# Attention products on parts of the matmul array, and the first layer's fold in plain float32

## The chip, the cores and the metric

The kernel runs on one core of one Trainium2 chip. The metric is device time in microseconds from launch to end, as a median over runs. A core has a matmul engine (TensorE: PE in the profile, its weight loads PEld), VectorE (DVE), ScalarE (ACT), GpSimd (POOL) and SyncE (SP), which here issues most DMAs; GpSimd issues the rest.

## The reference

Attention with landmarks for 4 batches of 8 heads, 576 tokens and 64 elements a head, then two MLPs over the 2304 tokens:

```python
q_lm, k_lm = means of q, k over 18 tokens each           # 32 landmarks
A  = softmax(scale * q    @ k_lm^T)                       # 576 x 32
Bm = softmax(scale * q_lm @ k_lm^T)                       # 32 x 32
C  = softmax(scale * q_lm @ k^T)                          # 32 x 576
Z  = Bm^T / (norm1(Bm) * norminf(Bm) + 1e-6)
for _ in range(6): Z = 2 * Z - Z @ Bm @ Z
attn = A @ Z @ C @ v
x = attn as (2304 tokens, 512)
x = (sigmoid(x @ w_gate) * (x @ w_val)) @ w_out           # 512 -> 1536 -> 512
x = h = x @ w_in2; (max(h, 0) + alpha * min(h, 0)) @ w_out2   # 512 -> 2048 -> 512
```

q, k and v come in float32, the MLPs' weights as 64-bit floats, which the kernel turns into float32 by integer operations on their bits.

## The kernel before

**Precision.** The MLP products run in float32r, a float32 format that TensorE takes in one go. Each operand is split into a high part and a rest (`split`: a copy on ScalarE, a subtraction on VectorE or GpSimd), and three products of such parts (`TERMS`) stand for one float32 product. The attention's products run in plain float32; each of them appears as two instructions in the trace.

**Attention.** A group is four heads of a batch (`j` = 0 or 1), a pair is two heads whose 64 elements fill the 128 partitions. `transposed` makes `qT` and `kT` of a pair: [(head, d), 576 tokens and 32 landmark means]. The scores of four heads are products over all 128 partitions: `blockdiag` spreads a pair's landmarks over the columns of its heads with the mask `lmask`, zeros elsewhere, and `pair_product` adds up the two pairs' products (`psb`, `psc`, `psa` in PSUM). `value_product` then multiplies by v, head after head, six token blocks each, into four strips of 32 partitions of `psv`. `newton` finds Z for four heads in four diagonal parts (`psz`), and multiplies it by C v (`psm`). The result goes through `lmask` into `mf`, which is block diagonal, and is split into `mhl`.

**The fold.** A @ (Z C v) @ W is computed as A @ (Z C v W). For batch b and chunk c of the weights (256 columns of w_gate and 256 of w_val), `fold` multiplies `mhl` by the chunk: per group, 3 terms by 2 pairs, six float32r products of 512 columns (`psf`). The result is split into `We[b, c, j]`. For batches 2 and 3 one `fold_two` per group and chunk does both: block-diagonal halves of one `mf` hold one batch each; batch 3's result is stored to DRAM (`we3d`) and fetched later.

**Weights of the first MLP.** A raw tile of 64-bit floats is loaded, `narrow` makes float32 of it (two operations on ScalarE and two on VectorE for w_gate and w_val, one and three for w_out), `split` makes `wconv`: 24 tiles of w_gate and w_val and 12 of w_out. The rest is subtracted on GpSimd, or on VectorE for the indices in `LO_DVE`. The 24 are stored to DRAM in split form (`wgvd`, issued by SP) and loaded again (`reload`, issued by GpSimd) for batch 1, and for batches 2 and 3. Split tiles live in 27 slots (`N_SLOT`).

**Order.** A loop of 96 steps `at` (24 for each batch) issues one `layer1` (`gv`, 12 products of 288 columns), one `layer2` of two steps before (`acc`, 12 products), and beside them conversions (batch 0), steps of the next batches' attentions, reloads (at `RELOAD_AT`), folds (at `FOLD_AT`) and, after the last fold, conversions of the second MLP's weights. A planner then orders each engine's instructions by their priority, which is mostly program order, and by when it reckons operands and buffers ready; the engines run them in that order. PSUM has eight banks: two for `gv`, four for `acc`, and two (`att`) for all attention products and folds; for batches 2 and 3 `layer1` uses `att` for odd f. The second MLP follows (`h`, `o`).

Of the kernel before, what the change touches and what calls it, by code (L numbers as in the profile page):

```python
# [21 lines left out]
def tile_landmark_attention_glu_prelu(  # L22
# [36 lines left out]
    RELOAD_AT, FOLD_AT = (16, 40), ((19, 20, 22, 23, 25, 27), (44, 46, 47, 49, 51, 53))  # L59
# [14 lines left out]
        (c, pr): dpool.tile([P, 2, NW], F32R, name=f"wgvd{c}_{pr}", tag=f"wgvd{c}_{pr}")  # L74
        for c in range(NCH)
        for pr in range(NK)
# [12 lines left out]
    lmask = cpool.tile([P, 2, 4, LM], F32, name="lmask")  # L89
    nc.gpsimd.memset(lmask, 0.0)  # L90
    for u in range(2):
        for hh in range(2):
            nc.gpsimd.memset(lmask[64 * hh : 64 * hh + 64, u, 2 * u + hh, :], 1.0)
    # eye[(h, l), l'] = 1 where l = l'
# [28 lines left out]
    def narrow(raw, to=None, act=False):  # L123
        """float32 of float64 bits, in place: sign, exponent less its bias' difference, 23
        mantissa bits. The high word, read as a float32, holds the exponent's upper eight bits in
        its own exponent: the scale takes 112 * 8 = 1023 - 127 off, and flushes what is too small."""
# [3 lines left out]
        if act:  # L130
            # the upper three of 16 bits, rounded to a whole number
# [26 lines left out]
    def load_pair_tok(src, b, pr, nm):  # L158
        """the two heads of a token side by side"""
# [14 lines left out]
    def pair_of(b, j, u):  # L174
        """the pair of heads in place u of group j; the last batch has them the other way round"""
        return 2 * j + (1 - u if b == B - 1 else u)
# [37 lines left out]
    def blockdiag(b, x, u, nm):  # L214
        t = apool.tile([P, 4, LM], F32, tag="bd", name=nm, bufs=7)
        (nc.gpsimd if b == 0 and nm[0] == "k" else nc.vector).tensor_tensor(
            out=t, in0=x[:, None, S:].to_broadcast([P, 4, LM]), in1=lmask[:, u], op=ALU.mult
        )
        return t.rearrange("p a l -> p (a l)")

    def pair_product(ps, lhsT, rhs, c0, c1):
        for u in range(2):
            nc.tensor.matmul(  # L223
                ps[:, : c1 - c0], lhsT=lhsT[u], rhs=rhs[u][:, c0:c1], start=(u == 0), stop=(u == 1)
            )

    def landmark_scores(b, j, ps_tile):
        """B of four heads, [(head, query landmark), key landmark]"""
        qT, kT, ql = att[b, j, "T"]
        ps = ps_tile("psb")  # L230
        pair_product(ps, ql, kT, S, S + LM)
# [18 lines left out]
    def att_landmarks(b, j, ps_tile):  # L250
        qT, kT = [], []
        for u in range(2):
            pr = pair_of(b, j, u)
# [4 lines left out]
        ql = [blockdiag(b, qT[u], u, f"ql{u}") for u in range(2)]  # L258
        att[b, j, "T"] = qT, kT, ql
# [5 lines left out]
    def value_scores(b, j, ps_tile):  # L265
        qT, kT, ql = att[b, j, "T"]
# [33 lines left out]
    def value_product(b, j, ps_tile):  # L300
        e, rd = att.pop((b, j, "e"))
        # C v, [(head, landmark), d]
# [12 lines left out]
        for u in range(2):  # L315
            pr = pair_of(b, j, u)
            vt = pre.pop(("v", pr)) if b == 0 else load_pair(v, b, pr, "vt")
            for hh in range(2):
                s = slice((2 * u + hh) * LM, (2 * u + hh + 1) * LM)
                for r in range(R):  # L320
                    nc.tensor.matmul(  # L321
                        ps[s, :D], lhsT=et[:, r, s], rhs=vt[:, hh, r * D : (r + 1) * D],
                        start=(r == 0), stop=(r == R - 1),
                    )
# [11 lines left out]
    def query_scores(b, j, ps_tile):  # L336
        qT, kT, ql = att[b, j, "T"]
        # A: all queries and landmark keys, to [(head, token), landmark]
# [598 lines left out]
```

## Time and profile before

| | |
|---|---|
| median of 3 runs | 941.32 us (941.22 to 946.16) |
| span of the profiled execution | 939.5 us |
| its own time, by the median less the span | 1.8 us around the span |
| TensorE, VectorE, ScalarE, GpSimd busy | 888.0, 564.9, 364.2, 187.7 us |
| DMA | 108.98 MB |

The span goes from the first to the last instruction of one execution on the chip. An engine's busy time is the union of its instructions. Matmuls are pipelined, so an instruction's own duration is longer than the time to the next one's start; the pieces of the chain of waits show the latter. "x12" counts instructions.

### The profile page before, as it was taken

To read this page: it belongs to the slowest core of one execution; us is meant where nothing else is said; L and a number is where in the kernel's file an instruction comes from. 1 tells how busy PE (TensorE), PEld (TensorE's weight loads), DVE (VectorE), ACT (ScalarE), POOL (GpSimd) and SP (SyncE) were. 2 spreads that over 40 slices of the span, in tenths; PEclk is the share of its full clock that TensorE was granted. 3 is DMA by queue.
4 is the path that set the end of the run, shared out by engine and by line. 5 is a ranking of instruction groups with operands and counts; after the bars stand their busy time and mean duration, and the time that the engine had idled before them with its cause. 6 is when DMAs were issued, how large, how long until landed. Compare 5 with 4: busy or idle time off the path is not lost.

```text
span 939.5 us, 14754 instructions
## 1 busy us (share of the span) xinstructions
PE 888.0 (95%) x5641; PEld 771.0 (82%) x5641; DVE 564.9 (60%) x1157; ACT 364.2 (39%) x763; POOL 187.7 (20%) x179
## 2 busy tenths in 40 slices
PE   5878888999999999989999889999999999999997
PEld 4557776899979889989899678888888888888896
DVE  5799989656656556695825994453434433443443
ACT  5656776336546545555425542121112111111111
POOL 3333235312100111044306442020002000000000
PEclk9959999999999999999999989999999999999999
DMA  9666777898533258663503541021003000100010
GB/s 270 173 225 232 244 233 251 182 304 231 139 77 99 69 157 273 224 211 118 172 1 115 160 135 45 1 59 31 1 1 80 0 1 12 45 1 0 14 33 23
DMA packets 81127, 108.98 MB, mean 116 GB/s; under 512 B 35216, under 2 KB 56736, under 8 KB 81056
## 3 DMA queue, kind: packets, MB, share of 16 engines
q1 hardware_dynamic: 74144, 82.87, 29.8%
q0 software_dynamic: 6912, 25.17, 9.1%
q8 instruction: 44, 0.72, 0.3%
q14 instruction: 27, 0.22, 0.1%
HBM read 82.85 MB, written 25.17 MB: 115 GB/s over the span
## 4 chain that ended last, share of the span: by engine, by line
PE 78%; issue 8%; DVE 7%; DMA 4%; POOL 2%; ACT 1%; SPq 0%; POOLq 0%; DVEq 0%; ACTq 0%
PE o L850 21%; PE h L832 21%; PE gv L637 12%; PE acc L656 11%; PE psf L589 3%; PE psf L607 2%; PE psv L321 2%; PE psa L223 2%; POOL wconv L115 1%; PE psc L223 1%; DMA raw<-in_moe_w_in_dram 1%; DVE raw L141 1%; PE psq L192 1%; DMA raw<-in_moe_w_out_dram 1%; PE psz L397 1%
## 5 line engine op out<-in xcount | busy, mean ns | idle before, releaser
L637 PE MATMUL gv<-A,we 128*128 128x288 f32 x1152 | 192.8, 306 | 4.6 <-ACT g L648 1.6
L832 PE MATMUL h<-x,w 128*128 128x512 f32 (+1 forms) x840 | 186.4, 371 | 5.2 <-DVE g L842 5.2
L656 PE MATMUL acc<-gs,wconv 128*128 128x288 f32 x1152 | 181.4, 300 | 7.9 <-DVE gs L115 3.5
L637 PEld LDWEIGHTS gv<-A,we 128*128 128x128 f32 x1152 | 165.8, 191 | 13.9 <-ACT g L648 2.4
L832 PEld LDWEIGHTS h<-x,w 128*128 128x128 f32 x840 | 149.6, 190 | 33.2 <-DVE g L842 5.5
L656 PEld LDWEIGHTS acc<-gs,wconv 128*128 128x128 f32 x1152 | 161.2, 188 | 14.5 <-DVE gs L115 5.2
L850 PE MATMUL o<-w,g2s 128*128 128x512 f32 x702 | 170.0, 389 | 0.0
L850 PEld LDWEIGHTS o<-w,g2s 128*128 128x128 f32 x702 | 131.0, 188 | 26.6
L114 ACT CAST g2s<-g 128x512 fp32r<-128x512 f32 (+1 forms) x80 | 46.3, 578 | 270.9 <-DVE g L842 270.9
L838 DVE TENSOR_SCALAR g<-h,alphaT 128x512 f32<-128x512 f32 (+1 forms) x80 | 55.7, 696 | 149.3 <-PE h L832 149.3
L115 DVE TENSOR_TENSOR g2s<-g,g2s 128x512 fp32r<-128x512 f32 (+1 forms) x80 | 54.9, 687 | 57.6 <-ACT g2s L114 57.2
L115 DVE TENSOR_TENSOR gs<-g,gs 128x288 fp32r<-128x288 f32 x96 | 56.4, 587 | 25.7 <-ACT gs L114 25.3
L115 POOL TENSOR_TENSOR x<-xr,x 128x512 fp32r<-128x512 f32 (+1 forms) x20 | 24.4, 1232 | 224.7 <-ACT x L114 224.7
L649 DVE TENSOR_TENSOR g<-g,gv 128x288 f32<-128x288 f32 x96 | 43.0, 448 | 40.8 <-PE gv L637 39.2
L114 ACT CAST gs<-g 128x288 fp32r<-128x288 f32 x96 | 41.7, 435 | 47.3 <-DVE g L649 47.1
L648 ACT ACTIVATE g<-gv 128x288 f32<-128x288 f32 x96 | 39.3, 409 | 52.5 <-PE gv L637 52.3
L115 POOL TENSOR_TENSOR wconv<-raw,wconv 128x512 fp32r<-128x512 f32 x26 | 42.0, 1621 | 71.5 <-ACT wconv L114 55.3
L138 DVE SCALAR_TENSOR_TENSOR raw<-raw 128x512 uint32<-128x512 uint32 x68 | 54.8, 812 | 1.2 <-ACT raw L129 0.3
L129 ACT ACTIVATE raw<-raw 128x512 f32<-128x512 f32 x68 | 46.7, 688 | 22.4 <-DMA raw<-in_moe_w_out_dram 9.3
L842 DVE SCALAR_TENSOR_TENSOR g<-h,g 128x512 f32<-128x512 f32 (+1 forms) x80 | 51.0, 637 | 2.6
L141 DVE SCALAR_TENSOR_TENSOR raw<-raw 128x512 uint32<-128x512 uint32 x60 | 50.8, 851 | 0.2
L579 POOL DMA_DIRECT2D wgv<-wgvd x48 | 25.8, 540 | 115.1 <-PE gv L637 48.1
(149 smaller groups left out, 990.2 us busy)
## 6 DMA issues: line engine op xcount, KB each, us to landing
wgv<-wgvd POOLq DMA_DIRECT2D x48, 512.0 KB, 6.0
raw<-in_moe_w_out_dram SPq DMA_DIRECT2D x28, 512.0 KB, 4.7
wgvd<-wconv SPq DMA_DIRECT2D x24, 512.0 KB, 5.5
raw<-in_moe_w_in_dram SPq DMA_DIRECT2D x16, 512.0 KB, 4.0
raw<-in_moe_w_gate_dram SPq DMA_DIRECT2D x24, 256.0 KB, 4.2
raw<-in_moe_w_val_dram SPq DMA_DIRECT2D x24, 256.0 KB, 4.6
x2d<-xs SPq DMA_DIRECT2D x32, 144.0 KB, 3.4
tkT<-in_k_dram SPq DMA_DIRECT2D x24, 144.0 KB, 4.6
```

Of the source, the lines that this page charges most:

```text
L114: nc.scalar.copy(dst[:, 0, :], src)
L115: (nc.gpsimd if lo == "pool" else nc.vector).tensor_tensor(out=dst[:, 1, :], in0=src, in1=f32(dst[:, 0, :]), op=ALU.subtract)
L129: nc.scalar.activation(w[:, :, 1], w[:, :, 1], AF.Copy, scale=2.0 ** -112)
L138: nc.vector.scalar_tensor_tensor(out=lo, in0=hi, scalar=0x80000000, in1=lo, op0=ALU.bitwise_and, op1=ALU.bitwise_or)
L141: nc.vector.scalar_tensor_tensor(out=lo if to is None else to.bitcast(U32), in0=hi, scalar=3, in1=lo, op0=ALU.logical_shift_left, op1=ALU. ...
L637: nc.tensor.matmul(ps[:, :HB], lhsT=We[b, c, j][:, a, 256 * i + P * s : 256 * i + P * s + P], rhs=att[b, j, "A"][half][:, e, :], start=(n ...
L649: nc.vector.tensor_tensor(out=g, in0=g, in1=pss[1][:, :HB], op=ALU.mult)
L656: nc.tensor.matmul(acc[m][:, :HB], lhsT=wout_sb[f][:, a, P * m : P * m + P], rhs=gs[:, e, :], start=(f == f0 and n == 0), stop=(f == f1 - ...
L832: nc.tensor.matmul(ps[:, :n], lhsT=w[:, a, kk], rhs=xs[:, e, kk, :n], start=(i == 0), stop=(i == 11))
L838: nc.vector.tensor_scalar(out=g[:, :n], in0=ps[:, :n], scalar1=0.0, scalar2=alphaT[:, f : f + 1], op0=ALU.min, op1=ALU.mult,)
L842: nc.vector.scalar_tensor_tensor(out=g[:, :n], in0=ps[:, :n], scalar=0.0, in1=g[:, :n], op0=ALU.max, op1=ALU.add)
L850: nc.tensor.matmul(acc, lhsT=gs[:, a, P * t : P * t + P], rhs=w2_out[f][:, e, :], start=(f == 0 and i == 0), stop=(f == NF2 - 1 and i == 2),)
```

## The change

Attention products use parts of the array, one head each. A head's operands lie on 64 partitions, its 32 landmarks fill 32 columns: `head_products` gives each of four heads a product of its own on another part. `HEADS[j]` now makes the groups so that the heads of the two groups lie on the eight different parts (64 rows by 32 columns). `blockdiag`, `lmask`, `pair_of`, `mf` and `mhl` are gone. `value_product` alternates between heads inside each token block.

Z C v times the chunk is now one plain float32 product per head, eight for a chunk, on eight parts, into two banks; the weights are kept in float32 and not split. One tile holds two pairs' weights, so a chunk has two tiles instead of four, and half the bytes are stored and reloaded. Each batch folds its own: batches 2 and 3 have separate folds (`FOLD_AT[1]`, `FOLD_AT[2]`), from the same reload; batch 3's result is still stored. Reloads run two chunks ahead.

```diff
-    RELOAD_AT, FOLD_AT = (16, 40), ((19, 20, 22, 23, 25, 27), (44, 46, 47, 49, 51, 53))
+    RELOAD_AT, FOLD_AT = (16, 40), (
+        (19, 20, 22, 23, 25, 27), (44, 46, 48, 50, 52, 54), (45, 47, 49, 51, 53, 55)
+    )
...
+    HEADS = [[(u, hh, 2 * u + (hh ^ j)) for u in range(2) for hh in range(2)] for j in range(2)]
...
-    def pair_product(ps, lhsT, rhs, c0, c1):
-        for u in range(2):
+    def head_products(ps, j, lm, x, c0, c1):
+        for u, hh, h in HEADS[j]:
+            d = slice(D * hh, D * hh + D)
             nc.tensor.matmul(
-                ps[:, : c1 - c0], lhsT=lhsT[u], rhs=rhs[u][:, c0:c1], start=(u == 0), stop=(u == 1)
+                ps[LM * h : LM * h + LM, : c1 - c0],
+                lhsT=lm[u][d, S:],
+                rhs=x[u][d, c0:c1],
+                start=True,
+                stop=True,
             )
...
-            pair_product(pc[half], ql, kT, half * HB, (half + 1) * HB)
+            head_products(pc[half], j, qT, kT, half * HB, (half + 1) * HB)
...
+        for r in range(R):
+            for u, hh, h in HEADS[j]:
+                s = slice(h * LM, (h + 1) * LM)
+                nc.tensor.matmul(
+                    ps[s, :D], lhsT=et[:, r, s], rhs=vt[u][:, hh, r * D : (r + 1) * D],
+                    start=(r == 0), stop=(r == R - 1),
+                )
...
+        pm = [ps_tile(f"psm{u}") for u in range(2)]
         cv = att[b, j, "Cv"]
...
+        for u, hh, h in HEADS[j]:
+            s = slice(h * LM, h * LM + LM)
+            nc.tensor.matmul(
+                pm[u][D * hh : D * hh + D, :LM], lhsT=cv[s], rhs=zt[s], start=True, stop=True
+            )
+        m = apool.tile([P, 2, LM], F32, tag="m", name="m", bufs=4)
         for u in range(2):
...
+            nc.vector.tensor_copy(m[:, u], pm[u][:, :LM])
+        att[b, j, "M"] = m
...
     def convert():
         kind, c, pr = conv.popleft()
-        t = ws_tile("wconv")
-        got = narrow(raws.pop((kind, c, pr)), act=kind == "w")
-        split(t, got, lo="dve" if c in LO_DVE else "pool")
+        raw = raws.pop((kind, c, pr))
         if kind == "o":
-            wout_sb[c] = t
+            t = wout_sb[c] = ws_tile("wconv")
+            split(t, narrow(raw), lo="dve" if c in LO_DVE else "pool")
             return
-        nc.sync.dma_start(out=f32(wgvd[c, pr]), in_=f32(t))
-        wgv[c, pr] = t
+        j, u = divmod(pr, 2)
+        if u == 0:
+            wgv[c, j] = ws_tile("wgv", dtype=F32)
+        t = wgv[c, j]
+        narrow(raw, t[:, u], act=True)
+        if u == 1:
+            nc.sync.dma_start(out=wgvd[c, j], in_=t)
         if pr == NK - 1:
+            take(0, c, fold(0, c, bank))
+
+    def reload(c):
+        if c < NCH:
             for j in range(2):
-                fold(0, c, j, bank)
...
+                wgv[c, j] = ws_tile("wgv", dtype=F32)
+                nc.gpsimd.dma_start(out=wgv[c, j], in_=wgvd[c, j])
...
+    def fold(b, c, ps_tile):
+        pss = [ps_tile(f"psf{j}") for j in range(2)]
         for u in range(2):
+            for j in range(2):
+                for v_, hh, h in HEADS[j]:
+                    if v_ != u:
+                        continue
+                    d = slice(D * hh, D * hh + D)
+                    nc.tensor.matmul(
+                        pss[j][LM * h : LM * h + LM],
+                        lhsT=att[b, j, "M"][d, u],
+                        rhs=wgv[c, j][d, u],
+                        start=True,
+                        stop=True,
+                    )
+        return pss
+
+    def take(b, c, pss):
+        for j in range(2):
+            We[b, c, j] = ws_tile("we")
+            split(We[b, c, j], pss[j])
+
+    def store_folded(c, pss):
+        for j in range(2):
+            st = apool.tile([P, NW], F32, tag="T", name="st", bufs=3)
+            (nc.vector.tensor_copy if j else nc.scalar.copy)(st, pss[j])
+            nc.sync.dma_start(out=we3d[c, j], in_=st)
...
             if at in RELOAD_AT:
                 reload(0)
+                reload(1)
             if at in FOLD_AT[0]:
                 c = FOLD_AT[0].index(at)
                 while (1, 1, "M") not in att:
                     next(nxt)
-                for j in range(2):
-                    fold(1, c, j, bank)
-                if c + 1 < NCH:
-                    reload(c + 1)
+                take(1, c, fold(1, c, bank))
+                reload(c + 2)
             if at in FOLD_AT[1]:
                 c = FOLD_AT[1].index(at)
                 for _ in nxt:
                     pass
-                for j in range(2):
-                    fold_two(c, j, bank)
-                if c + 1 < NCH:
-                    reload(c + 1)
-                else:
+                take(2, c, fold(2, c, bank))
+            if at in FOLD_AT[2]:
+                c = FOLD_AT[2].index(at)
+                store_folded(c, fold(3, c, bank))
+                reload(c + 2)
+                if c + 1 == NCH:
                     apool.release()
```

## Rows read from the trace of the kernel before

**Rows 1.** The page's summary: span, and TensorE's busy time, share and instructions.

```profile
span 939.5 us, 14754 instructions
...
PE 888.0 (95%) x5641; PEld 771.0 (82%) x5641; DVE 564.9 (60%) x1157; ACT 364.2 (39%) x763; POOL 187.7 (20%) x179
```

**Rows 2.** Stages: length; busy PE, PEld, DVE, ACT, POOL; clock; DMA share, GB/s.

```profile
0.00:44.00 44.00, 30.80 (x285) 24.07 (x285) 28.60 (x103) 25.51 (x62) 15.29 (x28) 1.00 0.85 236
44.00:165.00 121.00, 100.00 (x640) 84.89 (x632) 113.22 (x228) 81.70 (x168) 46.78 (x30) 0.89 0.71 231
165.00:400.00 235.00, 234.65 (x1976) 207.87 (x1977) 144.67 (x404) 119.70 (x271) 39.59 (x59) 1.00 0.63 175
400.00:520.00 120.00, 115.83 (x863) 114.19 (x862) 76.41 (x128) 58.40 (x126) 47.13 (x33) 1.00 0.39 125
520.00:560.00 40.00, 32.80 (x154) 26.99 (x153) 39.57 (x57) 20.43 (x36) 17.50 (x12) 0.91 0.52 160
560.00:939.50 379.50, 373.89 (x1739) 312.99 (x1737) 162.40 (x242) 58.49 (x104) 21.39 (x19) 1.00 0.08 21
```

**Rows 3.** VectorE by line, 44 to 165 us: count, busy us, mean ns, idle before.

```profile
L141 DVE SCALAR_TENSOR_TENSOR raw<-raw 128x512 uint32<-128x512 uint32 x34 | 29.0, 857 | 0.0
L138 DVE SCALAR_TENSOR_TENSOR raw<-raw 128x512 uint32<-128x512 uint32 x33 | 24.9, 761 | 0.1
...
L115 DVE TENSOR_TENSOR we<-psf,we 128x512 fp32r<-128x512 f32 x12 | 8.2, 683 | 1.3 <-ACT we L114 1.3
L115 DVE TENSOR_TENSOR wconv<-raw,wconv 128x512 fp32r<-128x512 f32 x10 | 6.7, 675 | 0.2 <-ACT wconv L114 0.2
...
L216 DVE TENSOR_TENSOR ql<-qT,lmask 128x128 f32<-128x128 f32 x4 | 3.4, 841 | 0.0
...
L454 DVE TENSOR_TENSOR mf<-psm,lmask 128x128 f32<-128x128 f32 x4 | 1.1, 284 | 0.0
L216 DVE TENSOR_TENSOR kl<-kT,lmask 128x128 f32<-128x128 f32 x4 | 1.0, 284 | 0.0
...
L115 DVE TENSOR_TENSOR mhl<-mf,mhl 128x256 fp32r<-128x256 f32 x2 | 0.8, 414 | 0.0
```

**Rows 4.** Instructions of tile `raw`, whole run: count, ns min/median/max, first and last start.

```profile
L138 DVE SCALAR_TENSOR_TENSOR raw<-raw x68: 644/684/1803, 21.5 to 561.5; 128x512 uint32<-128x512 uint32 x68
L141 DVE SCALAR_TENSOR_TENSOR raw<-raw x60: 670/684/1761, 24.8 to 563.3; 128x512 uint32<-128x512 uint32 x60
```

**Rows 5.** GpSimd by line, 44 to 165 us.

```profile
L115 POOL TENSOR_TENSOR wconv<-raw,wconv 128x512 fp32r<-128x512 f32 x24 | 39.4, 1648 | 69.0 <-ACT wconv L114 55.3 <-PE psv L321 10.8 <-DMA raw<-in_moe_w_out_dram 1.5
```

**Rows 6.** The chain of waits, 200 to 260 us: start, us, what.

```profile
209.83 1.94 PE psa L223 x8
...
221.84 1.62 PE acc L656 x12
...
225.30 2.22 PE psv L321 x48
227.52 2.97 PE psf L589 x12
```

**Rows 7.** TensorE's timeline in narrow windows: start, us, what (instructions that reach in).

```profile
35.83 0.31 PE L397 MATMUL psz<-rz 32*32 32x64 f32 x8
...
180.01 0.56 PE L656 MATMUL acc<-gs,wconv 128*128 128x288 f32 x3
180.50 0.32 PE L450 MATMUL psm<-zt,cv 32*64 32x32 f32 x8
180.74 0.79 PE L656 MATMUL acc<-gs,wconv 128*128 128x288 f32 x4
...
225.23 0.63 PE L321 MATMUL psv<-vt,et 96*32 96x64 f32 x8
...
225.53 0.58 PE L321 MATMUL psv<-vt,et 96*32 96x64 f32 x11
```

More of the change, by code (lines that the diff above doesn't have):

```diff
@@ L73, in tile_landmark_attention_glu_prelu @@
     wgvd = {
-        (c, pr): dpool.tile([P, 2, NW], F32R, name=f"wgvd{c}_{pr}", tag=f"wgvd{c}_{pr}")
+        (c, j): dpool.tile([P, 2, NW], F32, name=f"wgvd{c}_{j}", tag=f"wgvd{c}_{j}")
         for c in range(NCH)
-        for pr in range(NK)
+        for j in range(2)
     }
@@ L212, in transposed @@
         return x
[L214 to L219, printed above, removed]
-    def pair_product(ps, lhsT, rhs, c0, c1):
-        for u in range(2):
-            nc.tensor.matmul(
-                ps[:, : c1 - c0], lhsT=lhsT[u], rhs=rhs[u][:, c0:c1], start=(u == 0), stop=(u == 1)
+    def head_products(ps, j, lm, x, c0, c1):
+        for u, hh, h in HEADS[j]:
+            d = slice(D * hh, D * hh + D)
+            nc.tensor.matmul(
+                ps[LM * h : LM * h + LM, : c1 - c0],
[3 more added lines that the diff above has]
+                stop=True,
             )
     def landmark_scores(b, j, ps_tile):
-        qT, kT, ql = att[b, j, "T"]
+        qT, kT = att[b, j, "T"]
         ps = ps_tile("psb")
-        pair_product(ps, ql, kT, S, S + LM)
+        head_products(ps, j, qT, kT, S, S + LM)
         mx = apool.tile([P, 1], F32, tag="bmx", name="bmx", bufs=2)
@@ L252, in att_landmarks @@
         for u in range(2):
-            pr = pair_of(b, j, u)
+            pr = 2 * j + u
             kT.append(transposed(k, b, pr, f"kT{u}", ps_tile))
@@ L257, in att_landmarks @@
             yield
-        ql = [blockdiag(b, qT[u], u, f"ql{u}") for u in range(2)]
-        att[b, j, "T"] = qT, kT, ql
+        att[b, j, "T"] = qT, kT
         if b == 0:
@@ L265, in value_scores @@
     def value_scores(b, j, ps_tile):
-        qT, kT, ql = att[b, j, "T"]
+        qT, kT = att[b, j, "T"]
         mx = apool.tile([P, 3], F32, tag="mx", name="mx", bufs=2)
@@ L314, in value_product @@
         ps = ps_tile("psv")
[L315 to L324, printed above, removed]
+        vt = [
+            pre.pop(("v", pr)) if b == 0 else load_pair(v, b, pr, "vt")
+            for pr in (2 * j, 2 * j + 1)
+        ]
+        for r in range(R):
[5 more added lines that the diff above has]
+                )
         cv = apool.tile([P, D], F32, tag="cv", name="cv", bufs=2)
@@ L336, in query_scores @@
     def query_scores(b, j, ps_tile):
-        qT, kT, ql = att[b, j, "T"]
-        kl = [blockdiag(b, kT[u], u, f"kl{u}") for u in range(2)]
+        qT, kT = att[b, j, "T"]
         ta = apool.tile([P, S], F32, tag="T", name="ta", bufs=3)
@@ L342, in query_scores @@
             ps = ps_tile("psa")
-            pair_product(ps, kl, qT, half * HB, (half + 1) * HB)
+            head_products(ps, j, kT, qT, half * HB, (half + 1) * HB)
             nc.vector.transpose(out=ta[:, half * HB : (half + 1) * HB], in_=ps[:, :HB])
@@ L572, in convert @@
+        if u == 0:
[4 more added lines that the diff above has]
+            nc.sync.dma_start(out=wgvd[c, j], in_=t)
         if pr == NK - 1:
+            take(0, c, fold(0, c, bank))
+    def reload(c):
+        if c < NCH:
             for j in range(2):
-                fold(0, c, j, bank)
-    def reload(c):
-        for pr in range(NK):
-            wgv[c, pr] = ws_tile("wgv")
-            nc.gpsimd.dma_start(out=wgv[c, pr], in_=wgvd[c, pr])
@@ L581, in tile_landmark_attention_glu_prelu @@
-    We = {}
-    def fold(b, c, j, ps_tile):
-        mhl = att[b, j, "M"].rearrange("p a (u c) -> p a u c", u=2)
-        ps = ps_tile("psf")
-        n = 0
-        for a, e in TERMS:
-            for u in range(2):
-                nc.tensor.matmul(
-                    ps, lhsT=mhl[:, a, u], rhs=wgv[c, 2 * j + u][:, e, :],
-                    start=(n == 0), stop=(n == 5),
-                )
-                n += 1
-        we = ws_tile("we")
-        split(we, ps)
-        We[b, c, j] = we
@@ L598, in fold_two @@
-    def fold_two(c, j, ps_tile):
-        mhl = att[B - 1, j, "M"].rearrange("p a (u c) -> p a u c", u=2)
-        we = ws_tile("we")
-        st = apool.tile([P, NW], F32, tag="T", name="st", bufs=3)
-        for u in range(2):
-            ps = ps_tile("psf")
-            for n, (a, e) in enumerate(TERMS):
-                nc.tensor.matmul(
-                    ps, lhsT=mhl[:, a, u], rhs=wgv[c, 2 * j + u][:, e, :],
-                    start=(n == 0), stop=(n == 2),
-                )
-            s0, s1 = slice(64 * u, 64 * u + 64), slice(64 - 64 * u, 128 - 64 * u)
-            nc.scalar.copy(we[s0, 0, :], ps[s0])
-            nc.vector.tensor_tensor(
-                out=we[s0, 1, :], in0=ps[s0], in1=f32(we[s0, 0, :]), op=ALU.subtract
-            )
-            (nc.vector.tensor_copy if u else nc.scalar.copy)(st[s1], ps[s1])
-        We[B - 2, c, j] = we
-        nc.sync.dma_start(out=we3d[c, j], in_=st)
+                wgv[c, j] = ws_tile("wgv", dtype=F32)
@@ L699, in convert_w2 @@
         split(w2_slot(i), staged[i] if i in staged else narrow(load_w2(i)), lo="pool")
-    al_raw = apool.tile([NF2, P], F32, tag="bd", name="al_raw", bufs=7)
+    al_raw = apool.tile([NF2, P], F32, tag="bd", name="al_raw", bufs=1)
     nc.sync.dma_start(out=al_raw, in_=alpha.rearrange("(f p) -> f p", p=P))
@@ L796, in tile_landmark_attention_glu_prelu @@
                 take_stored(f // 2)
-            if qpool is not None and at > FOLD_AT[1][-1]:
+            if qpool is not None and at > FOLD_AT[2][-1]:
                 if at % W2_EVERY == 0:
```

33 lines of the change are left out of this document (removed).

## The prediction, made before the changed kernel ran

> **What bounds the kernel now.** I read the page's summary first [rows 1]: TensorE is busy for 95% of a 939.5 us span, so the first guess is that only TensorE's work counts. The busy time by stage [rows 2] corrects that. From 560 us on the second MLP keeps TensorE at 374 of 379.5 us, and the change doesn't touch it. From 165 to 400 us TensorE is busy for 234.65 of 235 us: what is taken off TensorE there comes off the time. From 44 to 165 us, where the first layers' weights are converted, VectorE is busy for 113.2 of 121 us (94%) and TensorE for 100, so VectorE sets the pace. Before 44 us nothing is full. From 400 to 560 us the second MLP's weights are converted; the change leaves that work alone.
>
> So three sums are wanted: VectorE's in 44:165, TensorE's in 165:400, and a small one before 44 us. The profiled span and the 941.32 us median differ by 1.8 us of launch around the span; I subtract from 939.5 and add 1.8 back.
>
> **The weight stage, 44:165.** Gone from VectorE [rows 3]: the low half of a converted tile for 8 of the 10 `wconv` rows (the other two are w_out's, which are still split), 8 x 0.675 = 5.4 us; the masked copies `ql` 3.4 and `kl` 1.0; the split of `mhl` 0.8; the four `mf` products (1.1) turn into four copies of a quarter of the width, whose price lies between nothing and the same 0.28, and I take 0.2: 0.3 saved. Together 10.9 us. `narrow` keeps its VectorE operations and only writes elsewhere.
>
> Then what GpSimd costs VectorE. The two shift-and-or operations have a median of 0.684 us over the whole run [rows 4] and means of 0.857 and 0.761 in this stage [rows 3], with maxima of 1.8: 34 x 0.173 + 33 x 0.077 = 8.4 us over the median. GpSimd's 24 `wconv` subtractions [rows 5] run in the same stretch, and 16 of those 24 are of gate and value weights, which vanish. If the excess goes with them in proportion, 5.6 us; the ends are 0 and 8.4. VectorE is then left with 113.2 - 10.9 - 5.6 = 96.7 us, and at today's 94% the stage takes 103 us: 18 us less. The ends: 94 us of stage (all excess gone, no idle time), a gain of 27, and a gain of 8, if something else holds the stage at 113.
>
> What is next in line there? ScalarE loses 24 copies and has 82 of 121 us today, so not it. DMA moved 231 GB/s x 121 us = 28 MB [rows 2]; the stored weights shrink from 24 x 0.5 to 12 x 0.5 MB, 22 MB stay, 95 us at that rate. TensorE's 100 us hold waits for the splits. DMA and VectorE thus end up close together, which is why I don't take more. SP's queue also gets lighter: half as many stores `wgvd` stand between the loads of raw weights, and a store no longer waits for a GpSimd subtraction.
>
> **TensorE, 165:400.** First the units. Twelve `acc` instructions of 288 columns follow one another in 1.62 us [rows 6], 135 ns each, so a 512-column float32r one takes 240 ns; a fold of 12 in 2.97 agrees. A plain float32 product appears as two instructions: `psa`, 8 in 1.94 us, gives 242 ns for 288 columns, or 0.43 us for 512 and 0.86 us for a whole product.
>
> *Folds.* Here 144 `psf` instructions (72 for batch 1, 72 for batches 2 and 3 at once) cost 144 x 0.24 = 34.6 us. In their place come 18 folds of eight float32 products, each on 64 rows and 32 columns of the array, no two on the same part. The whole gain hangs on how many run at once. Four 32-row parts of Newton's `psz` take 0.31 us for 8 instructions, and `psm`, whose parts share columns two by two, 0.32 [rows 7]; in sequence, at the 46 ns that `psv` needs for 64 columns (48 in 2.22 us [rows 6]), 8 `psz` would need 0.37 us for their starts alone. And `psv`, eight instructions in 0.63 us while they share a 32-column strip, manages eleven in 0.58 where the next head's strip joins in [rows 7]. So parts with other rows, and parts with other columns, overlap. Eight at once over 512 columns isn't shown. Bounds: 0.86 us all together, 6.9 us one by one; I take 0.86, as every row with separate parts shows overlap.
>
> Into and out of the small parts there is a price: between `acc` instructions, `psm` starts 0.09 us late, and after it the first two `acc` lose another 0.10 [rows 7]. With the end of the small products themselves, 0.3 us per excursion. A fold is 1.16, say 1.2 us, in one piece, and 2.3 in two pieces (its two banks not free together, other work put between). The planner can cut them so; I take a third cut: 12 x 1.2 + 6 x 2.3 = 28 us, a saving of 7 (one piece: 13; all in two: -7).
>
> *C v.* Five groups of 48 instructions at 2.22 us. Heads now alternate, so four strips overlap: 2.22/4 = 0.56, say 0.7. Saved 5 x 1.5 = 7.5 us (at least 3, if only two strips overlap as shown).
>
> *Scores.* Eight pairs of halves at 1.94 us [rows 6] become four parts at once per half: 2 x 0.485 + 0.3 to 0.6 = 1.3 to 1.6; 1.4 taken, saved 8 x 0.54 = 4.3 us.
>
> *Against it.* A fold takes both `att` banks, and they come free only after a copy on ScalarE and a 0.683 us subtraction `we<-psf` on VectorE [rows 3], one bank after the other. After the folds of batch 2 the next `gv` of odd f wants those banks. Other TensorE work can be put in between; I charge 3 us over 18 folds (0 if always covered, 18 x 0.7 = 13 if never). Sum: -7 - 7.5 - 4.3 + 3 = -16 us.
>
> **Before 44 us.** Two `psv` groups and four score pairs are shortened by up to 5 us, but TensorE has only 30.8 busy of 44 us [rows 2] and VectorE stands between: -2 (0 to -5). **After 400 us.** Work on the second weights starts two steps later; VectorE has 44 us of idle time in 400:520, so 0.
>
> **Sum.** -2 - 18 - 16 = -36: span 903.5, time 905 us.
>
> **Rivals.**
> - *Folds cut up and waiting for banks.* All 18 in two pieces, 41 us instead of 28, and bank waits of 10 instead of 3: +20, 925 us. For it: the folds of before are already broken by other instructions wherever a bank is late. Against it: half as many reloads, two chunks ahead, so the operands should all be there. Chance 0.17.
> - *The weight stage doesn't shrink*, because loads, not VectorE, hold it: 905 + 18 = 923 us. For it: 231 GB/s [rows 2]; against: raw tiles are freed earlier. Chance 0.08.
> - *Row parts of one bank take turns.* Both row halves of a group write to one bank. Then a fold is two rounds, 2.0 us or more, instead of 1.2: 18 x 0.86 = +15.5, and the scores save nothing and pay for the excursion: +7. Together 927 us. `psz` and `psm` put four row parts into one bank in 0.31 and 0.32 us [rows 7], which speaks against it. Chance 0.05. The Trainium skill's page "TensorEngine Tiling (Array Packing)", section Restrictions and Gotchas, Gotcha 1, states this rule: different row tiles cannot access the same PSUM bank at the same time. By that rule this rival would be the forecast; the trace disagrees with it at 64 columns and below, and has nothing longer.
> - *Slower: the parts hardly overlap.* With the long plain float32 streams each fold costs its passes: four times the work per column against three float32r products on full parts. One by one a fold is 6.9 us, 18 of them 124 against 35 now, and the scores double from 15.5 to 31: over 1,010 us. The point from which it decides: my folds average 1.56 us, and the 36 us are used up at 1.56 + 36/18 = 3.6 us a fold, which is two parts at a time (4 x 0.86 + 0.3 = 3.7). For it: no row with eight parts, or with streams this long. Against it: every row with separate parts. Chance 0.07.
>
> **How the numbers follow.** The forecast holds 0.63 and spans 886 to 918: by its ends, the most favourable sum (-5 - 27 - 26) is 883, little above which I cut. The first three rivals fill 918 to 935. The range 886 to 932 leaves out the slower case (0.07), a part of the cut-up case (0.07) and a better one (0.05). What this kernel's measurement tells from no change is about 0.5%, 4.7 us. Faster 0.88; same 0.04 (the first rival with a stage that doesn't shrink); slower 0.08.
>
> **What would show it.** Right: a fold's 16 `psf` instructions start within 0.1 us of one another by eights and end in about 1.2 us; `psv` takes 0.7 us for 48; 44:165 shrinks to about 103 us with VectorE still over 90% and its `raw` operations near 0.70 us; 165:400 shrinks by some 16 us and TensorE stays full. Wrong: `psf` starts 0.4 us apart (no overlap); `gv` waiting for `we` (banks); the weight stage at 120 us with raw loads ending the waits; long pieces between the halves of a fold. The prediction fails most if overlap fails, and by less if the planner cuts the folds.

## The result and the profile after

The changed kernel takes 902.81 us (median of 4 runs, 901.25 to 906.15) against 942.2 before (now of 4 runs too): ratio 0.9588, 95% interval 0.9563 to 0.9612. The forecast was 905. The profiled execution took 901.25 us, with a span of 899.5.

The page's summary and the stages, cut where the same work ends (columns as in [rows 2]):

```profile
span 899.5 us, 15163 instructions
...
PE 851.9 (95%) x5969; PEld 703.6 (78%) x5969; DVE 526.5 (59%) x1097; ACT 335.9 (37%) x715; POOL 144.7 (16%) x130
```

```profile
0.00:44.00 44.00, 26.62 (x349) 15.73 (x349) 30.39 (x104) 27.29 (x67) 14.83 (x20) 0.89 0.86 247
44.00:150.00 106.00, 95.39 (x748) 67.09 (x748) 93.53 (x213) 67.71 (x140) 19.52 (x15) 0.95 0.70 214
150.00:360.00 210.00, 208.22 (x2131) 166.49 (x2131) 119.14 (x357) 102.77 (x241) 22.37 (x32) 1.00 0.43 126
360.00:480.00 120.00, 114.75 (x850) 113.85 (x849) 80.86 (x130) 59.24 (x128) 48.80 (x34) 0.99 0.42 130
480.00:520.00 40.00, 32.72 (x158) 27.17 (x157) 39.63 (x57) 20.23 (x37) 17.47 (x13) 0.91 0.53 160
520.00:899.50 379.50, 374.16 (x1740) 313.24 (x1738) 162.93 (x242) 58.68 (x104) 21.73 (x19) 1.00 0.08 21
```

Against [rows 1, 2]: TensorE is still at 95% of its span, which says nothing about the 40 us that went. From 360 us on, every stage has its old length and nearly its old busy times (VectorE 80.9 us from 360 to 480, 76.4 in the same stage before); the 40 us went before that. The weight stage with its batch 0 folds and the full stretch after it have lost 15 and 25 us in these cuts. The cut at 150 us is 6 us generous to the first: batch 0's last fold ended at 164.2 us before and ends at 144.0 now, so by that mark it is 20 and 20, where I had 2 + 18 and 16.

In the weight stage, VectorE by line and GpSimd (columns as in [rows 3, 5]):

```profile
L134 DVE SCALAR_TENSOR_TENSOR raw<-raw 128x512 uint32<-128x512 uint32 x31 | 22.8, 746 | 0.3 <-ACT raw L129 0.3
L137 DVE SCALAR_TENSOR_TENSOR wgv<-raw 128x512 uint32<-128x512 uint32 x22 | 16.5, 762 | 0.0
L137 DVE SCALAR_TENSOR_TENSOR raw<-raw 128x512 uint32<-128x512 uint32 x12 | 9.0, 763 | 0.0
...
L111 DVE TENSOR_TENSOR wconv<-raw,wconv 128x512 fp32r<-128x512 f32 x2 | 1.4, 676 | 0.0
```

```profile
L111 POOL TENSOR_TENSOR wconv<-raw,wconv 128x512 fp32r<-128x512 f32 x10 | 14.9, 1491 | 76.4 <-ACT wconv L110 40.2 <-PE gv L613 18.4 <-DMA vt<-in_v_dram 17.7
```

GpSimd's subtractions fell from 24 to 10, and VectorE's raw operations from means of 0.761 and 0.857 us to 0.746 and 0.76. VectorE is at 88% of this stage, no longer at 94%, so it doesn't set the pace alone; experiment 6 looks for what else does.

TensorE's granted clock is at its lower level (0.5 in the rows, 1.2 of 2.4 GHz) for a part of this stage in both kernels: from 43.8 to 67.7 us before, from 38.0 to 51.7 now (and for some 3 us once more in either). It fell while TensorE was busy for 2.6 of 4 us (40 to 44) before and for 0.8 of 4 us (36 to 40) now, and rose while it was busy for 3.5 of 4 us (64 to 68) and for 4.0 of 4 (48 to 52). Before, VectorE was busy for 23.8 of the 24 us from 44 to 68, so no row says that the clock held the stage there; what the shorter stretch is worth, no run separates.

TensorE's timeline around one fold, first all of it, then in a window that ends at 312.66 us (a row holds the instructions that reach into the window, with the time to the end of the last):

```profile
312.23 0.42 PE L632 MATMUL acc<-gs,wconv 128*128 128x288 f32 x2
312.59 1.09 PE L575 MATMUL psf<-wgv,m 64*32 64x512 f32 x16
313.61 0.67 PE L613 MATMUL gv<-A,we 128*128 128x288 f32 x3
...
312.59 0.66 PE L575 MATMUL psf<-wgv,m 64*32 64x512 f32 x8
```

Eight products of 512 columns run together: the first eight instructions all begin within the 0.07 us up to 312.66 and have ended 0.66 us after the first start; the other eight, each product's second instruction, begin from 313.04 on. The fold is over in 1.02 us, from 312.59 to the next `gv` at 313.61. The chain of waits over steps of batches 2 and 3 shows what lies around it:

```profile
303.81 1.02 PE psf L575 x16
304.83 1.79 PE gv L613 x12
306.62 1.61 PE acc L632 x12
...
321.35 0.13 PE acc L632
321.48 1.56 PE psf L575 x16
323.04 1.78 PE gv L613 x12
```

No fold of batches 1 to 3 has other work between its products. The twelve `gv` behind a fold take 1.79 us where twelve `acc` take 1.61: that is the way out of the small parts. In a fold of 1.56 us (four of the twelve of batches 2 and 3) two products start and the other six wait half a microsecond for the second bank; in the window up to 321.9 us only four instructions have begun, two for each of the two products. One fold of batch 1 takes 2.10 us in the same way, its others 1.02 to 1.35:

```profile
321.41 1.05 PE L575 MATMUL psf<-wgv,m 64*32 64x512 f32 x4
```

The shares of the chain over steps 18 to 56 (194 us) give the terms' sizes:

```profile
by line: PE gv L613 34.6%; PE acc L632 33.0%; PE psf L575 11.8%; PE psq L188 3.8%; PE psa L215 3.0%; DMA tqT<-in_q_dram 2.9%; PE psz L393 2.9%; PE psc L215 2.4%; PE psv L318 2.2%; PE pse L303 1.4%; PE psm L439 1.1%; PE psbb L393 0.6%; PE ps
```

18 folds: 22.9 us (28 forecast, 34.6 before). Scores: 5.4% or 10.5 us for eight pairs of halves, 1.3 each (1.4 forecast). C v: 4.3 us for four groups, 1.07 each (0.7 forecast). The 2.9% of a load of q are a piece of 5.65 us in the chain, but no idle time of TensorE: it had other work for all but 0.56 us of it.

### The profile page after: what moved, and what is told of

The parts are those of the page before. It is cut to its first block, busy times and chain, and to the rows that moved or that the text cites. A ratio compares the mean times of both kernels' runs of the same rounds, so it can differ in the third digit from the quotient of the medians.

```text
span 899.5 us, 15163 instructions
## 1 busy us (share of the span) xinstructions
PE 851.9 (95%) x5969; PEld 703.6 (78%) x5969; DVE 526.5 (59%) x1097; ACT 335.9 (37%) x715; POOL 144.7 (16%) x130
## 4 chain that ended last, share of the span: by engine, by line
PE 81%; DVE 8%; DMA 4%; issue 3%; ACT 1%; POOL 1%; SPq 1%; DVEq 0%; POOLq 0%; ACTq 0%
PE o L826 22%; PE h L808 22%; PE gv L613 14%; PE acc L632 13%; PE psf L575 4%; DVE raw L134 2%; DVE raw L137 1%; DMA raw<-in_moe_w_val_dram 1%; PE psa L215 1%; PE psq L188 1%; DMA tv<-in_v_dram 1%; PE psz L393 1%; DVE raw L131 1%; PE psc L215 1%; DVE wgv L137 1%
## 5 line engine op out<-in xcount | busy, mean ns | idle before, releaser
L613 PE MATMUL gv<-A,we 128*128 128x288 f32 x1152 | 190.1, 304 | 6.3 <-ACT g L624 4.1
L632 PE MATMUL acc<-gs,wconv 128*128 128x288 f32 x1152 | 185.5, 302 | 7.9 <-DVE xs L723 4.0
L613 PEld LDWEIGHTS gv<-A,we 128*128 128x128 f32 x1152 | 161.0, 189 | 37.3 <-issue 22.9
L111 DVE TENSOR_TENSOR gs<-g,gs 128x288 fp32r<-128x288 f32 x96 | 51.7, 539 | 26.9 <-ACT gs L110 26.2
L134 DVE SCALAR_TENSOR_TENSOR raw<-raw 128x512 uint32<-128x512 uint32 x68 | 55.7, 825 | 1.6 <-ACT raw L129 0.6
L575 PE MATMUL psf<-wgv,m 64*32 64x512 f32 x384 | 45.7, 620 | 0.8 <-DVE wgv L137 0.4
L111 DVE TENSOR_TENSOR we<-psf,we 128x512 fp32r<-128x512 f32 x36 | 23.7, 685 | 18.1 <-ACT we L110 18.1
L137 DVE SCALAR_TENSOR_TENSOR raw<-raw 128x512 uint32<-128x512 uint32 x36 | 32.1, 898 | 0.2
## 6 DMA issues: line engine op xcount, KB each, us to landing
x2d<-xs SPq DMA_DIRECT2D x32, 144.0 KB, 2.3
tkT<-in_k_dram SPq DMA_DIRECT2D x24, 144.0 KB, 4.1
```

The costliest lines, as they stand in the source:

```text
L111: (nc.gpsimd if lo == "pool" else nc.vector).tensor_tensor(out=dst[:, 1, :], in0=src, in1=f32(dst[:, 0, :]), op=ALU.subtract)
L134: nc.vector.scalar_tensor_tensor(out=lo, in0=hi, scalar=0x80000000, in1=lo, op0=ALU.bitwise_and, op1=ALU.bitwise_or)
L137: nc.vector.scalar_tensor_tensor(out=lo if to is None else to.bitcast(U32), in0=hi, scalar=3, in1=lo, op0=ALU.logical_shift_left, op1=ALU. ...
L575: nc.tensor.matmul(pss[j][LM * h : LM * h + LM], lhsT=att[b, j, "M"][d, u], rhs=wgv[c, j][d, u], start=True, stop=True,)
L613: nc.tensor.matmul(ps[:, :HB], lhsT=We[b, c, j][:, a, 256 * i + P * s : 256 * i + P * s + P], rhs=att[b, j, "A"][half][:, e, :], start=(n ...
L632: nc.tensor.matmul(acc[m][:, :HB], lhsT=wout_sb[f][:, a, P * m : P * m + P], rhs=gs[:, e, :], start=(f == f0 and n == 0), stop=(f == f1 - ...
```

## Experiments

Two-part theory, as forecast: half of the gain from array parts that run at once on a full TensorE, half from a lighter VectorE in the weight stage. Rivals: all from the array, or all from the weights. Times are medians; ratios are to the kernel before, on the same chip.

**1. Four parts instead of eight.**

```diff
-    HEADS = [[(u, hh, 2 * u + (hh ^ j)) for u in range(2) for hh in range(2)] for j in range(2)]
+    HEADS = [[(u, hh, 2 * u + hh) for u in range(2) for hh in range(2)] for j in range(2)]
```

> The changed kernel with both groups of heads on the same four parts of the array (no exchange of columns between the groups). Two-part theory (half of the gain from parts that run at once on a full TensorE, half from VectorE's lighter weight stage): a fold needs two rounds, 1.9 us instead of 1.05, so 18 folds in the full stretch cost 18 x 0.86 = 15 us more, and the six of batch 0 up to 5 us: 917 to 923 us against 902.8. Weights theory (the gain is all from the unsplit weights, folds are covered anyway): 903 to 907 us. In the trace the second group's four instructions should start 0.43 us behind the first group's rather than 0.03.

919.77 us, ratio 0.9761 (0.9728 to 0.9793). The same fold on the timeline:

```profile
312.85 1.93 PE L575 MATMUL psf<-wgv,m 64*32 64x512 f32 x16
314.71 0.53 PE L613 MATMUL gv<-A,we 128*128 128x288 f32 x2
```

From its start to the next `gv` it takes 1.86 instead of 1.02 us, 0.84 more; 18 times that is 15 of the 17 us. The second group's products begin 0.88 us behind the first's, after both instructions of each, and not 0.43 as I had expected. Folds are on the path, and the eight-fold overlap is worth what its rows say. The weights theory falls.

**2. The attention's parts alone, on the kernel before.** `pair_product` and `blockdiag` make room for four products by heads, and C v alternates between heads; split weights and float32r folds stay.

```diff
-            pair_product(ps, kl, qT, half * HB, (half + 1) * HB)
+            head_products(ps, kT, qT, half * HB, (half + 1) * HB)
...
-        for u in range(2):
-            for hh in range(2):
-                for r in range(R):
+        for r in range(R):
+            for u, hh, h in HEADS:
```

> The kernel before with the attention's scores and C v on parts of the array, the masked copies gone, but the split weights, the masked Z C v and the float32r folds as before. Two-part theory: C v saves about 1.2 us for each of 6 groups in the full stretch, the scores 4, small products 2, the masked copies 4 us of VectorE in the weight stage, the first attention 2 to 4: 942 less 17 to 21, 921 to 925 us. Weights theory: 936 to 942 us. Array theory (all of the gain from the array, half of it from the folds): 920 to 925 as well, so this run doesn't tell that one apart; the next does.

941.56 us, ratio 0.999 (0.9962 to 1.0017): nothing, where I expected 17 to 21. The products did get shorter (`psv`, 48 in 0.81 us in the rows below). The chain of waits and the stages show TensorE waiting instead:

```profile
228.76 0.81 PE psv L318 x48
229.57 1.60 PE psf L585 x6
231.17 0.37 SPq L162
231.54 0.04 issue
231.59 10.79 DMA tqT<-in_q_dram
```

```profile
220.00:240.00 20.00, 16.73 (x163) 14.60 (x162) 13.74 (x38) 11.82 (x26) 5.33 (x9) 1.00 0.94 276
240.00:260.00 20.00, 17.48 (x125) 14.18 (x126) 9.71 (x30) 7.71 (x14) 3.88 (x5) 0.83 0.53 133
```

A load of q for the next attention takes 10.8 us to land while reloads keep the DMA engines at 94%, and its transposes stand in TensorE's queue ahead of other work: TensorE idles for 5.8 us in front of them. More was lost at the end of the weight stage. The last operand of batch 0's last fold was ready at 152.4 us, 10 us earlier than before (162.7), but the attention of batch 1 had been queued ahead of that fold, which ended at 167.2 us, before at 164.2. The chain goes through the scores of that attention to the fold:

```profile
161.74 0.72 PE psc L219 x8
...
163.42 0.60 ACT e L285 x2
164.02 0.14 issue
164.15 3.04 PE psf L585 x12
```

**3. The attention undone on the changed kernel,** the complement: masked copies and scores over 128 partitions are back, C v goes head after head; unsplit weights and folds stay.

```diff
-            head_products(ps, j, kT, qT, half * HB, (half + 1) * HB)
+            pair_product(ps, kl, qT, half * HB, (half + 1) * HB)
...
-        for r in range(R):
-            for u, hh, h in HEADS[j]:
+        for u, hh, h in HEADS[j]:
+            for r in range(R):
```

> The complement of the attention-alone run: the changed kernel with its attention put back (masked copies, scores as products over all 128 partitions, C v head after head), keeping unsplit weights, eight-part folds and halved stores and reloads. Collision theory (attention alone gained nothing because its time went into other waits: a chain of attention steps queued before the last fold of batch 0, and a load of q that took 10.8 us between the reloads): without those the attention parts are worth their sum here, 12 us of TensorE in the full stretch and 2 to 5 before it, so 915 to 920 us. Worthless theory (attention was covered in either kernel): 902 to 905 us.

922.7 us, ratio 0.9804 (0.9761 to 0.9846): 20 us, of which the profiled executions show 16 by step 56 (table below), near the 14 to 17 of the collision theory. Nearly the same edit is worth nothing on the kernel before. "Covered in either kernel" falls.

**4. Attention alone, with half the bytes reloaded.**

```diff
-            nc.gpsimd.dma_start(out=wgv[c, pr], in_=wgvd[c, pr])
+            nc.gpsimd.dma_start(out=wgv[c, pr][:, 0], in_=wgvd[c, pr][:, 0])
```

> The attention-alone kernel with reloads of the high halves only, 256 KB instead of 512 KB a tile; in the folds of batches 1 to 3 the high half stands in the place of the low one, so the low parts of those weights are left out and the instructions stay the same in number and shape. Collision theory (attention alone lost its gain to loads of q late behind the reloads, and 6 us to the order at the end of the weight stage): the wait of TensorE for q goes, 931 to 936 us. If the lost time lies elsewhere: 939 to 942 us.

933.2 us, ratio 0.9894 (0.9843 to 0.9946): 8 us less than with full reloads. The same two stretches are full:

```profile
220.00:240.00 20.00, 20.00 (x184) 17.85 (x177) 14.44 (x45) 12.58 (x29) 2.91 (x6) 1.00 0.69 168
240.00:260.00 20.00, 19.99 (x226) 16.78 (x224) 13.81 (x45) 12.98 (x26) 3.53 (x5) 1.00 0.25 61
```

So on the kernel before, the collision with the reloads took 8 us of the attention's gain. The changed kernel has half the reloads and not this wait; whether the one is the cause of the other, experiment 6 asks. My prediction had no term for it.

**5. The splitting put back, and its pieces.** All of it, as work without use:

```diff
         narrow(raw, t[:, u], act=True)
+        old = apool.tile([P, 2, NW], F32R, tag="old", name="old", bufs=2)
+        split(old, t[:, u], lo="dve" if c in LO_DVE else "pool")
```

> The changed kernel with the splitting of each gate and value tile put back as work without use: a ScalarE copy and a subtraction on GpSimd (16) or VectorE (8) into a scratch tile. Two-part theory: VectorE gets 5.4 us back and some 4 us of slowing by GpSimd, and GpSimd's 16 subtractions at 1.4 us; nothing waits for the result but the next scratch tile, so the weight stage grows by 6 to 10 us: 909 to 913 us. Array theory: the stage is held by loads and TensorE, so 902 to 905 us. The stores stay halved.

921.61 us, ratio 0.9783 (0.9763 to 0.9804): 18.8 us, twice what I expected here. The prediction's 18 us for the stage held the masked copies and the split of `mhl` as well; for this splitting alone it had 5.4 and 5.6 us of VectorE. The array theory falls too. The stage with VectorE's main rows:

```profile
44.00:166.00 122.00, 104.18 (x764) 71.11 (x764) 109.06 (x226) 80.92 (x165) 43.58 (x31) 0.88 0.62 186
```

```profile
L134 DVE SCALAR_TENSOR_TENSOR raw<-raw 128x512 uint32<-128x512 uint32 x31 | 23.5, 769 | 0.0
L137 DVE SCALAR_TENSOR_TENSOR wgv<-raw 128x512 uint32<-128x512 uint32 x23 | 18.8, 825 | 0.0
L111 DVE TENSOR_TENSOR gs<-g,gs 128x288 fp32r<-128x288 f32 x15 | 10.9, 728 | 0.0
...
L111 DVE TENSOR_TENSOR old<-wgv,old 128x512 fp32r<-128x512 f32 x8 | 6.2, 780 | 2.3 <-ACT old L110 2.2
```

VectorE has 15.5 us more to do than in the changed kernel, 6.2 of them its own eight subtractions; the rest is in operations that take longer, and in the longer stretch. Then one piece at a time. GpSimd's 16 subtractions:

```diff
+        if c not in LO_DVE:
+            old = apool.tile([P, NW], F32, tag="old", name="old", bufs=2)
+            nc.gpsimd.tensor_tensor(out=old, in0=t[:, u], in1=t[:, u], op=ALU.subtract)
```

> The changed kernel with 16 subtractions of a gate or value tile on GpSimd put back alone, into scratch tiles, without the ScalarE copies and without VectorE's eight. Slowing theory (a GpSimd operation that starts inside a VectorE one holds it up by 0.5 to 1.1 us): the three-operand raw operations of VectorE in the weight stage go from a mean of 0.75 to 0.80 us or more, 5 to 8 us in all, and the time to 907 to 911 us of the 921.6 with all of the splitting. If only VectorE's and ScalarE's own work counts: 902 to 904 us.

906.92 us, ratio 0.9628 (0.9589 to 0.9666): 4.1 us. VectorE's operations slow down, which is the price forecast at 5.6 us:

```profile
L134 DVE SCALAR_TENSOR_TENSOR raw<-raw 128x512 uint32<-128x512 uint32 x31 | 25.1, 821 | 0.0
L137 DVE SCALAR_TENSOR_TENSOR wgv<-raw 128x512 uint32<-128x512 uint32 x23 | 19.2, 844 | 0.0
```

The mean of one line wanders from run to run (0.834 us for L134 with ScalarE's copies alone, the next run, which has no subtraction more). A count shows it better. From 44 us to the end of batch 0's last fold, 8 of these 62 operations ran beside an arithmetic operation of GpSimd in the changed kernel, and 24 of 63 here. Those took 1.03 and 1.00 us on average; the others 0.682 and 0.681, and none of them more than 0.695. Of the 24, 13 began while GpSimd's operation was already running, and 11 of these took over 0.85 us; the expectation has the order the other way round.

ScalarE's 24 copies:

```diff
+        old = apool.tile([P, NW], F32R, tag="old", name="old", bufs=2)
+        nc.scalar.copy(old, t[:, u])
```

> The changed kernel with 24 ScalarE copies of the gate and value tiles put back alone, into scratch tiles, without any subtraction. With all of the splitting back the time rose by 18.8 us, with GpSimd's subtractions alone by 4.1; VectorE's eight are worth at most 5.4 us of its time. Queue theory (a copy waits for VectorE's last operation on its tile, and ScalarE's next raw operations stand behind it): 8 to 12 us more, 911 to 915 us, with ScalarE's copy waiting 10 us in all for VectorE. If only VectorE's work counts: 902 to 904 us, and the rest of the 18.8 us comes from the three together.

902.27 us, ratio 0.9565 (0.9522 to 0.9608): nothing; 24 copies of 0.62 us are covered. The queue theory falls. Copies 0 and GpSimd 4 leave some 14 us of the 18.8 to VectorE's eight subtractions (6.2 us) and to the three together; that they add up so was not tried further.

**6. Bytes.** Every reload once more, into a scratch tile:

```diff
+                again = apool.tile([P, 2, NW], F32, tag="again", name="again", bufs=2)
+                nc.gpsimd.dma_start(out=again, in_=wgvd[c, j])
```

> The changed kernel with every reload followed by a second one of the same 512 KB into a scratch tile that nobody reads: 25 MB of reloads again, as before. Collision theory: loads of q, k and v for the next batch land late between 160 and 240 us and TensorE waits for them, as in the attention-alone run: 907 to 911 us. If halving the reloads is worth nothing: 902 to 904 us.

915.76 us, ratio 0.9718 (0.968 to 0.9756), 13 us, but not where I looked: 10 of them are lost before step 16. The DMA issues of its weight stage (KB each, us to landing) say why; 11 of the scratch loads, which need no free slot, went out already there:

```profile
again<-wgvd POOLq DMA_DIRECT2D x11, 512.0 KB, 4.5
```

In the stretch where I had looked, from batch 0's last fold to step 56, the run loses 1.6 us, and TensorE doesn't idle once there in front of a transpose of q or k. So the collision theory isn't borne out: the other 13 scratch loads don't bring the wait of experiment 2 back, and it is not shown that the halved reloads are what spares the changed kernel that wait.

What the 11 early loads cost in the weight stage asks for another run: each store twice, which puts 6.3 MB back into that stage and nothing else:

```diff
             nc.sync.dma_start(out=wgvd[c, j], in_=t)
+            nc.sync.dma_start(out=wgvd2[c, j], in_=t)
```

> The changed kernel with every converted gate and value tile stored twice, to two places in DRAM: 24 stores of 512 KB as before, 6.3 MB more between 40 and 145 us, and nothing more of reloads or arithmetic. Loads theory (raw loads hold the weight stage beside VectorE; the run with reloads twice lost 10 us there, where 11 of its scratch loads had gone out early): 8 to 12 us more by the first step of the last chunk, 910 to 915 us. VectorE theory: 902 to 904 us.

916.84 us, ratio 0.9722 (0.9668 to 0.9777): 14 us, by bytes and issues alone. Its stage (to 160 us) and the longest wait of its chain:

```profile
44.00:160.00 116.00, 93.67 (x677) 66.86 (x677) 91.25 (x195) 62.22 (x129) 16.64 (x12) 0.87 0.78 247
```

```profile
140.12 10.31 DMA tqT<-in_q_dram
```

VectorE now has 91 us of work in 116: it doesn't hold the stage. A late load of q does at its end, for an attention step queued ahead of a fold, as in experiment 2; in the whole stage (its last fold ends at 163.4 us) TensorE idles for 12.1 us in front of transposes, and in the changed kernel's for none. Whether bytes or places in SP's queue cost more, one run bears on: the twelve stores of the version below issued by GpSimd instead of SP.

> The version with the shift on ScalarE for all tiles (895.5 us) and the twelve stores of converted gate and value tiles issued by GpSimd instead of SP. Queue-order theory (a store on SP waits for VectorE's last operation on its tile, and loads of raw weights and of q, k, v stand behind it): the weight stage loses 2 to 5 us, 890 to 893 us. Bytes theory (the stores cost by their 6.3 MB, whoever issues them): 894 to 898 us.

897.18 us, ratio 0.9495 (0.9457 to 0.9533), against 895.47 for that version: no gain. SP's queue isn't the cost of the halved stores; of the doubled ones this doesn't tell.

**7. Less for VectorE.** The shift of w_out's raw tiles on ScalarE, and then of all tiles of 64-bit weights:

```diff
-            split(t, narrow(raw), lo="dve" if c in LO_DVE else "pool")
+            split(t, narrow(raw, act=True), lo="dve" if c in LO_DVE else "pool")
```

> The changed kernel with the shift of the twelve w_out tiles on ScalarE (as it is for gate and value tiles) instead of VectorE: 12 x 0.42 to 0.5 = 5 to 6 us less for VectorE in the weight stage, 8 us more for ScalarE. If VectorE still sets that stage's pace (two-part theory): 897 to 899 us. If loads and TensorE hold it by now: 902 to 904 us.

900.3 us, ratio 0.956 (0.9537 to 0.9582): 2.5 us, half of what VectorE was relieved of. The interval overlaps the changed kernel's own (0.9563 to 0.9612), so the gain isn't certain. It would fit two holders of one stage: take from one, and the other has the rest.

> The changed kernel with the shift on ScalarE for all tiles of 64-bit weights, those of the second MLP too: 32 x 0.42 us more off VectorE, in two stretches in which VectorE is at 99% and TensorE waits 4 and 7 us (360 to 380 and 480 to 520 us in the changed kernel). If VectorE sets those: 2 to 6 us less than with the w_out tiles alone, 894 to 898 us. If ScalarE's extra work or GpSimd's splits hold them: 899 to 902 us.

895.47 us, ratio 0.9504 (0.947 to 0.9537), and the shortest of all: 7 us under the changed kernel, 46 under the one before. Of the 4.7 us between the two profiled executions 4.1 lie behind step 56, where the second MLP's weights are converted; the weight stage is as long as in the changed kernel. Its stretch at the start of the second MLP (to 516 us, as that MLP starts earlier) has VectorE at 32 of 36 us, where the changed kernel has 39.63 of 40:

```profile
480.00:516.00 36.00, 31.04 (x151) 25.95 (x150) 32.00 (x42) 24.93 (x46) 17.51 (x12) 0.95 0.58 177
```

**Where the runs lose their time.** From the profiled executions, in us: from the start to the end of batch 0's last fold, from there to the first `gv` product of step 56, and the rest, which none of these edits is meant to touch and which still differs by up to 8 us.

| | to the last fold of batch 0 | to step 56 | rest |
|---|---|---|---|
| before | 164.2 | 228.1 | 547.1 |
| changed | 144.0 | 207.2 | 548.3 |
| four parts (1) | 147.7 | 221.7 | 551.0 |
| attention alone (2) | 167.2 | 223.0 | 549.5 |
| attention undone (3) | 147.5 | 219.8 | 554.7 |
| attention alone, half reloads (4) | 167.3 | 215.1 | 548.1 |
| splitting put back (5) | 158.1 | 209.7 | 551.0 |
| reloads twice (6) | 154.6 | 208.8 | 551.3 |
| stores twice (6) | 163.4 | 205.9 | 547.6 |

What the parts of the array are worth lies mainly in the second column, what splitting and stored bytes cost in the first.

## Why the prediction was right

*The start and the weight stage: -20 forecast, -20 measured.* The size came out right, in part by luck. I had VectorE's work in the stage fall to 96.7 us and fill 94% of 103 us; from 44 to 144 us it is 88.0 us, 88% of the stage. One error made up for the other, and the sign that I named, VectorE still over 90%, isn't there. Of the parts, ScalarE's copies at nothing held, and GpSimd's slowing of VectorE was 4.1 us where I had 5.6. The splitting as a whole costs 18.8 us when it is put back, more than the 11 us of VectorE that I had for it; some 14 of them stay open between VectorE's subtractions and the three together. What was incomplete is the holder. I wrote that DMA and VectorE "end up close together" and charged only VectorE; experiment 6 shows 14 us for the stored bytes that the change takes off. The two don't add up: with the splitting back batch 0's last fold ends at 158.1 us, with the stores doubled at 163.4, against 144.0 in the changed kernel and 164.2 before, so either one brings most of the stage back. The rival in which loads hold the stage was wrong about the time, as far as experiment 6 tells, because the change lightens the loads as well.

*The full stretch: -16 forecast, -20 measured.* Folds took 22.9 us instead of 28 and 3 more for late banks: I took a third to be cut in two, and none was; the waits for late banks, of which the four folds of 1.56 us and the one of 2.10 are the largest, are inside the 22.9. The way in and out of the parts, 0.3 us, was right in size: 0.18 is seen in the twelve `gv` behind each fold. C v was 1.07 us a group and not 0.7, scores 1.3 and not 1.4. Counted from each product's start to the next one's, between batch 0's last fold and 400 us (now 360), folds fell from 34.8 to 22.8 us, C v from 13.0 to 5.3, scores from 14.7 to 10.7 and the attention's other products from 24.5 to 21.7: 26.5 us. `gv` and `acc` take 6.7 us more there, for which the way out of the small parts (18 x 0.18 = 3.2), 22 more instructions in this stretch (3.0) and TensorE's idle time (2.0 us, 0.7 before) are enough. Most of the 4 us beyond the forecast are the cuts that didn't come.

*The rivals.* Cut folds occur in batch 0, where tiles come one by one; four-instruction pieces take 0.98 us, as long as a whole fold, so the price of that rival was right; only its place is the stage in which TensorE isn't full (89.6 us busy from 44 to 144). Row parts of one bank don't take turns: each bank of a fold gets products of both row halves, and all eight begin within 0.07 us. The rule of the Trainium skill, page "TensorEngine Tiling (Array Packing)", section Restrictions and Gotchas, Gotcha 1 (different row tiles cannot access the same PSUM bank simultaneously), doesn't hold here for writes of 512 columns to different partitions of a bank. Weak overlap: none; with four parts it would have been 17 us worse, as the price of two rounds said (15.5 us for 18 folds, in the rival of row parts).

*What I missed* is that the attention's gain hangs on what else is queued and loaded. The forecast counted shortened products on a full TensorE as time. On the kernel before that fails: they turned into other waits (experiment 2), 8 us of them into a load behind full reloads (experiment 4). On the changed kernel it holds (experiment 3), so the total was right under a condition that the prediction didn't see. Why the wait stays away there is open, as doubled reloads didn't bring it back (experiment 6).

## What to carry to other kernels

A full TensorE pays back shortened products only as long as nothing else is due at the old pace: when compute shrinks, look for the next load that stands in the same in-order queue, and count the bytes around it. Where two resources end a stage at nearly the same time, either can be shown to cost most of what was gained by being put back, and the prices don't add. Plain float32 products on eight separate parts of the array, 1.02 us for eight of 512 columns, beat three float32r terms of twelve instructions (2.97 us) and need no split at all.

## What the runs showed of the hardware

Eight 64-row, 32-column parts ran plain float32 streams of 512 columns at once with little loss: the second instructions follow the first by 0.45 us, and the fold's 1.02 us is little over the 0.86 us that the prediction works out for one such product. Both row halves wrote to one bank meanwhile. A switch from small parts back to the whole array cost the next twelve products 0.18 us. VectorE's three-operand integer operations took 0.68 us, and at most 0.695, where no arithmetic operation of GpSimd ran beside them, and 1.00 us on average beside one (63 operations of the run with 16 subtractions back).
